# Moving the last routing steps and the zero fills in the planned order of a fused attention and expert kernel

## The chip, the cores and the metric

The kernel runs on one core of a Trainium2 chip. The metric is the device time in microseconds of one execution, 954.01 us before the change (median of three runs, 954.0 to 954.9). A profile of another execution of the same kernel shows where the time lies.

## What is computed

Three stages follow one another. The first is a recurrent attention with a complex decay per position, the second a mixture of eight experts of which every token goes to two, the third a feed-forward layer whose hidden value is the maximum of three products.

```python
# 4 batches, 8 heads, 768 positions, head size 48
scale = minimum(mag, 0.999) / (mag + 1e-06)
for t in range(768):
    S_re, S_im = ar * S_re - ai * S_im + k[t] v[t]^T, ar * S_im + ai * S_re
    y[t] = q[t] S_re
x = y as 3072 tokens x 384
noisy = x @ w_gate + log1p(exp(x @ w_noise)) * noise
top2, weights = two largest of noisy, softmax over them
out[token] += weight * (relu(x @ w1[e]) @ w2[e])        # 8 experts, 384 -> 1024 -> 384
h = maximum(maximum(x @ u1, x @ u2), x @ u3)            # 384 -> 768
result = h @ w_out
```

## The kernel before

The 3072 tokens are 24 chunks of 128, worked on in six sets of four chunks. For each set the decay (`gates`) is turned into cumulated magnitudes and angles: logarithms and exponentials with one table of ScalarE (tag `e1`), a matmul that cumulates and two exponentials of it, r and ri (tags `g`, `ex`), then arctangent and sine with another table (tags `t1`, `t2`, `f`, `sin`). For each chunk (`chunk`) q and k are scaled (`a0`, `a`), transposed (`b`), multiplied and masked (`d`), multiplied with v and the carried state (`c`, `s`, `l`); the output rows become fp16 pairs `xhl`, and logits of the gate come from the same product (`f_`).

Routing (`route`, tag `rt`) works on groups of two chunks, twelve groups. It finds the two experts of a token, counts tokens per expert with `acc`, and ends with `r2b3` (L900), which casts the row numbers into `sl`. A scatter (L940, tag `scat`, on POOL's queue) then writes the 128 rows of a chunk into the experts' row blocks in DRAM, two scatters per chunk, so four per group and 48 in all. Before any scatter, the row blocks are filled with zeros by eight fills of two transfers each on SP's queue (`zero_fill`, L972, tag `zf`).

The first pass of the experts (`first_pass`) takes 384 rows of each expert from chunks 0 to 11. Its weights (tag `xw`) are loaded once the `sl` of the fifth group is written, its rows are read by transposing transfers (tag `xx`, L1006) once the scatters of the first six groups are done. It is interleaved with the attention of chunks 12 to 23. The second pass (`second_pass`) takes the other 432 rows of each expert and needs all scatters. After it the third stage runs (`combine`, `hidden`, `last`), in a fixed order.

What sets the order up to the third stage is a planner inside the program, the class `Order`. Each step is added with a cost per engine, the keys it reads and writes, and a priority: the number of its chunk (or pass) plus an offset for its tag from the table `P["o"]`. The planner simulates the engines, their buffers and the ScalarE table phases: of the steps that are ready first it emits the one with the lowest priority. The order of emission is the order of instructions on each engine and each queue. On the chip only real data dependences make an engine wait; keys that exist for the planner alone shape the order, not the waits. Buffers limit it too: `xhl` has eight, `rw`, the scratch of routing, three.

The lines to watch are L900 (`sl`), L940 (scatters), L976 and L979 (zero fills), L437 (most ScalarE steps), L777 and L760 (state and output rows), L1037 and L1057 (first pass), L1098 and L1124 (second pass), L1507 (gathers of the third stage), L1557 and L1583 (its matmuls).

Of the kernel before, what the change touches and what calls it, by code (L numbers as in the profile page):

```python
# [32 lines left out]
    bufs=dict(bk=5, vg=2, wst=4, w1=1, w2=1, xa=2, hh=1, ya=2, ar=1, ai=1, iv=2, tn=1, r=1, ri=1, cs=3, fa=3,  # L33
           lam0=2, lam=6, lx=2, q=2, k=2, v=4, qr=3, kr=1, qc=2, kc=2, qt=2, kt=2, pm=2, xt=1, xhl=8, zp=1, fr=1,
           fh=4, car=1, sc=1, py=1, ps=1, lr=1, rw=3, w1b=1, w2b=1, raw=2, ua=1, vh=4, ch=1, cl=1),
    o=dict(load=-278.44, e1=-80.82, g=-44.76, ex=27.33, lam=13.6, t1=124.93, t2=491.73, f=-344.44, sin=58.57,
           tc=-621.27, qkv=204.29, v=669.22, a0=-227.64, a=84.82, b=-227.33, d=-609.19, c=-58.23, s=-165.23,
           l=90.33, f_=14.8, rt=-247.65, scat=-246.48, zf=803.51, gate=-153.95, noise=149.71, xw=125.96, xx=-312.17,
           x1=-201.57, xe=-424.5, x2=17.72, xo=-1189.75, yw=61.09, yx=-118.02, y1=-594.47, ye=185.57, y2=-134.08,
           yo=454.95, uw=1011.11, ue=388.46, pl=276.27, z=-83.6, mr=971.2),  # L40
    sets=[4, 4, 4, 4, 4, 4],
    e1ph=[0, 1, 2, 3, 4, 5],
    groups=[2, 2, 2, 2, 2, 2, 2, 2, 2, 2, 2, 2],
# [4 lines left out]
    a0=["dve"],  # L48
    a=["dve"],
# [11 lines left out]
    latpe=0.2,  # L61
    same=0.15,
    eps=0)
WARM = 20


class Order:
# [9 lines left out]
        self.bufs = bufs  # L77
        self.ops = []

    def add(self, fn, eng, prio, r=(), w=(), hold=(), table=None, phase=None, xfer=0.0, since=0, two=False, prev=None, mode=None, issues=1, after=()):  # L80

        self.ops.append(dict(fn=fn, eng=eng, prio=prio[0] + P["o"][prio[1]], r=list(r), w=list(w), hold=list(hold), table=table,
                             phase=phase, xfer=xfer, since=since, two=two, prev=prev, mode=mode, issues=issues, after=after))
        return len(self.ops) - 1

    def link(self):
# [32 lines left out]
    def run(self, emit, lat, latpe, same, eps):  # L121
# [14 lines left out]
        at = dict(self.BEGIN)  # L136
        hw = dma = awake = pe = port = done = 0.0
        mode = None
        need = {}
        for o in ops:  # L140
            if o["phase"] is not None:
                need[o["phase"]] = need.get(o["phase"], 0) + 1
        phase = 0
# [6 lines left out]
        while todo:  # L150
            best = None
            for e, ns in pool.items():
                cands = []
                for n in ns:
                    o = ops[n]
                    x = rdy[n][e]
                    if e in ("DVE", "POOL") and o["two"]:
                        x = max(x, port)
                    sw = False
                    if o["since"] > phase + (not need.get(phase, 0)):  # L160
                        continue
                    if o["table"] is not None:
                        if o["phase"] is not None and o["phase"] != phase:
                            if o["phase"] != phase + 1 or need.get(phase, 0):
                                continue
                            sw = True
                        elif o["phase"] is None and phase % 2:
                            if phase < end_phase or need.get(phase, 0):
                                continue
                            sw = True  # L170
                    ok = True
                    for t in o["tiles"]:
                        if t not in live:
                            f = free[self.CLASS.get(t[0], t[0])]
                            if not f:
                                ok = False
                                break
                            x = max(x, f[0][0])
                    if not ok:
                        continue  # L180
                    if sw:
                        x -= self.LOAD
                    cands.append((max(x, at[e]), o["prio"], n, sw))
                if not cands:
                    continue
                m = min(cands)[0]
                c = min((c for c in cands if c[0] <= m + eps), key=lambda c: (c[1], c[2]))
                if best is None or (c[0], c[1]) < best[0]:
                    best = (c[0], c[1]), e, c
            assert best, "too few buffers"  # L190
            _, e, (x, _, n, sw) = best
            o = ops[n]
# [6 lines left out]
            if e == "PE":  # L199

                if o["mode"] != mode:
                    mode = o["mode"]
# [5 lines left out]
                pe = x + cost  # L208
            end = x + cost
            at[e] = end  # L210
            if e in ("DVE", "POOL") and o["two"]:
                port = end
            if o["xfer"]:
# [35 lines left out]
def tile_kernel(ctx, tc, q, k, v, a_re, a_im, w_gate, w_noise, noise, w1, w2,  # L249
# [10 lines left out]
    E = w_gate.shape[1]  # L260
# [25 lines left out]
    ex = ctx.enter_context(tc.tile_pool(name="ex", bufs=1, side="left"))  # L286
# [89 lines left out]
    sl = const.tile([128, NI, 2], I32, name="sl")  # L376
# [7 lines left out]
    O = Order(BF)  # L384
# [437 lines left out]
    def route(gi, i0, n):  # L822
        sl_ = slice(i0, i0 + n)
        at, d = 0, {}
# [4 lines left out]
        def pr(x=0):  # L829
            return i0 + n - 1 + x, "rt"  # L830
# [91 lines left out]
        g = ("rt", i0, None)  # L922
# [6 lines left out]
        O.add(r1d, {"DVE": 0.08}, pr(1), r=[("rw", i0, 3)], w=[("rv", i0, "d")], hold=[("rw", i0)], two=True)  # L929
        O.add(r2b, {"DVE": 0.1}, pr(), r=[pp_], w=[("rw", i0, 8)])  # L930
        for m, (f, c) in enumerate(((r2b1, 0.2), (r2b2, 0.2), (r2b3, 0.08))):
            O.add(f, {"DVE": c}, pr(), r=[("rw", i0, m + 8)], w=[("sl", i0, None) if m == 2 else ("rw", i0, m + 9)], two=m == 0)
        O.add(r3, {"ACT": 0.1}, pr(1), r=[("rv", i0, "d")], w=[("rv", i0, 0)], hold=[("rw", i0)], table=0)
        for m, f in enumerate((r3b, r3c, r3d, r3e)):
            O.add(f, {"DVE": 0.08}, pr(1), r=[("rv", i0, m)], w=[("rv", i0, m + 1)], hold=[("rw", i0)], two=m in (0, 3))
# [15 lines left out]
        for j in range(n):  # L951
            for t in range(2):
                O.add(scatter(i0 + j, t), {"POOL": 1.26}, (i0 + j, "scat"),
                      r=[("sl", i0, None), ("xhl", i0 + j, None)] + [("xz", e, None) for e in range(E)], w=[("xs", i0 + j, t)], xfer=0.27)
# [382 lines left out]
    def combine_first(weighed):  # L1337
# [27 lines left out]
        for k in range(KD):  # L1365
# [17 lines left out]
          w=[("car", 1, None)])  # L1383
# [36 lines left out]
    def more_rows(e_, j):  # L1420
# [4 lines left out]
          w=[("wst", "no", None)])  # L1425
# [206 lines left out]
```

## Time and profile before

| | |
|---|---|
| median of three runs | 954.01 us (954.0 to 954.9) |
| span of the profiled execution, first to last instruction | 983.5 us |
| mean granted TensorE clock in it | 0.979 |
| busy: PE, DVE, ACT, POOL | 930.6, 574.0, 476.0, 139.0 us |
| instructions | 16814 |

The profiled execution is a run of its own, with a span 29.5 us above the median of the timed runs; the page gives no other time for it. PE is TensorE, DVE VectorE, ACT ScalarE, POOL GpSimd, and SP the queue that issues most transfers. A busy time counts from an instruction's start to its (for PE modelled) end. [...] "Idle before" is how long an engine did nothing ahead of an instruction, with what released it; "issue" means that nothing the profile shows was waited for, "remote" that the releaser isn't shown.

### The profile page before, as it was taken

Reading aid. Unit: us, or ns where it says so; the run is one execution under the profiler, and the core shown is the slowest. Engines: PE = TensorE matmul, PEld = TensorE weight load, DVE = VectorE, ACT = ScalarE, POOL = GpSimd, SP = SyncE. Lnnn points to the kernel's source line nnn. Section 1 sums busy time; section 2 is a strip of 40 time slices with the busy share of each in tenths; the row PEclk is TensorE's granted clock in tenths of the full one; section 3 lists DMA queues with packets and bytes.
Section 4 is the critical chain, followed back from the end, with each engine's and each line's share of the span. In section 5 each row is a group of like instructions: output and inputs, shape, how many; then the busy total and the mean of one; then the engine's idle time right before and its main releaser. Section 6 shows DMA issues by size and latency. Waiting matters only on the chain. (4 is left out here: it accounts for less than half of the span.)

```text
span 983.5 us, 16814 instructions
## 1 busy us (share of the span) xinstructions
PE 930.6 (95%) x6312; PEld 586.8 (60%) x6312; DVE 574.0 (58%) x1252; ACT 476.0 (48%) x922; POOL 139.0 (14%) x197
## 2 busy tenths in 40 slices
PE   3989778899999999899999999999799999999998
PEld 1868667787666766455555555555675445454544
DVE  5989748999655756565887764454344332424231
ACT  7998748978644556243445444333233132313221
POOL 0101442422001000520100000000433030300000
PEclk9999969999999999899999999999999999999999
DMA  9999848796765546379888785552335141502000
GB/s 150 211 214 271 195 120 159 182 194 165 191 185 168 158 153 201 123 223 312 253 253 238 209 208 155 147 141 79 107 116 142 40 133 36 140 25 78 25 9 33
DMA packets 247902, 150.98 MB, mean 154 GB/s; under 512 B 196488, under 2 KB 235528, under 8 KB 247816
## 3 DMA queue, kind: packets, MB, share of 16 engines
q1 hardware_dynamic: 241672, 130.98, 52.1%
q0 software_dynamic: 6144, 18.88, 6.4%
q8 instruction: 50, 0.82, 0.4%
q14 instruction: 36, 0.29, 0.1%
HBM read 89.78 MB, written 45.81 MB: 138 GB/s over the span
## 5 line engine op out<-in xcount | busy, mean ns | idle before, releaser
L437 ACT ACTIVATE hh<-bk 128x384 f16<-128x384 f32 (+1 forms) x128 | 64.6, 508 | 85.4 <-PE bk L1098 43.2
L985 ACT ACTIVATE w<-wst 128x768 f16<-128x768 f32 (+1 forms) x77 | 71.1, 932 | 59.6 <-PE bk L1057 23.3
L1057 PE MATMUL bk<-w,hh 128*128 128x384 f16 x576 | 98.6, 331 | 1.3 <-issue 1.3
L1037 PE MATMUL bk<-xa,w 128*128 128x384 f16 x576 | 99.6, 326 | 0.0
L987 DVE SCALAR_TENSOR_TENSOR w<-wst,w 128x768 f16<-128x768 f32 (+1 forms) x77 | 81.4, 1068 | 12.4 <-ACT w L985 11.5
L1571 ACT ACTIVATE th<-mx 128x512 f16<-128x512 f32 (+1 forms) x42 | 23.8, 568 | 127.2 <-DVE mx L1570 125.5
L1057 PEld LDWEIGHTS <-hh 128*128 128x128 f16 x576 | 56.7, 99 | 41.6 <-issue 6.5
L1124 PEld LDWEIGHTS <-hh 128*128 128x128 f16 x576 | 55.0, 98 | 40.3 <-issue 5.0
L1037 PEld LDWEIGHTS <-w 128*128 128x128 f16 x576 | 55.1, 98 | 34.4 <-issue 1.4
L1569 DVE TENSOR_TENSOR mx<-mx,u 128x512 f32<-128x512 f32 (+1 forms) x42 | 25.6, 610 | 62.5 <-PE u L1557 62.5
L1507 POOL DMA_INDIRECT yg<-ys_rows,sy x42 | 43.5, 1036 | 119.6 <-ACT za L1511 104.4
L940 POOL DMA_INDIRECT xs_rows<-xhl,sl x48 | 55.4, 1154 | 35.5 <-issue 18.5
L443 DVE COPY ya<-bk 128x384 f32<-128x384 f32 x37 | 20.6, 558 | 67.7 <-PE bk L1057 45.7
L732 PE MATMUL sc<-qt,kt 96*128 96x128 f32 x384 | 55.4, 287 | 4.5 <-issue 1.8
L732 PEld LDWEIGHTS sc<-qt,kt 96*128 96x128 f32 x384 | 49.3, 197 | 12.1 <-issue 4.1
L1098 PE MATMUL bk<-xa,w1b 128*128 128x432 f16 x288 | 53.2, 346 | 0.0
L1098 PE MATMUL bk<-xa,w 128*128 128x432 f16 x288 | 53.2, 346 | 0.0
L1107 DVE SCALAR_TENSOR_TENSOR hh<-bk,hh 128x432 f16<-128x432 f32 x64 | 37.9, 605 | 24.9 <-ACT hh L437 24.8
L1124 PE MATMUL bk<-w2b,hh 128*128 128x384 f16 x288 | 48.4, 326 | 0.0
L1124 PE MATMUL bk<-w,hh 128*128 128x384 f16 x288 | 48.4, 326 | 0.0
L1570 DVE TENSOR_TENSOR mx<-mx,u 128x512 f32<-128x512 f32 (+1 forms) x42 | 25.7, 611 | 37.4 <-PE u L1557 33.2
L1513 DVE SCALAR_TENSOR_TENSOR z<-yg,wt,za 128x384 f32<-128x384 f32 x22 | 12.8, 614 | 58.7 <-ACT za L1511 52.2
(204 smaller groups left out, 2012.7 us busy)
## 6 DMA issues: line engine op xcount, KB each, us to landing
wst<-in_moe_w_dram SPq DMA_DIRECT2D x45, 512.0 KB
wst<-in_moe_w_dram SPq DMA_DIRECT2D x60, 384.0 KB
xs_rows<-wst SPq DMA_DIRECT2D x8, 1152.0 KB
ys_rows<-ya SPq DMA_DIRECT2D x48, 192.0 KB
raw<-in_moe_w_dram SPq DMA_DIRECT2D x9, 768.0 KB
ar<-in_a_re_dram SPq DMA_DIRECT2D x24, 192.0 KB
ai<-in_a_im_dram SPq DMA_DIRECT2D x24, 192.0 KB
q<-in_q_dram SPq DMA_DIRECT2D x24, 192.0 KB
```

The source lines that it names most:

```text
L437: nc.scalar.activation(o, i, f, **kw)
L732: nc.tensor.matmul(tl("sc", (i, g))[:, j, :], tl("kt", i)[:, h, :], tl("qt", i)[:, h, :], start=True, stop=True)
L940: ins = nc.gpsimd.indirect_dma_start(out=xs, out_offset=bass.IndirectOffsetOnAxis(ap=sl[:, i, t:t + 1], axis=0), in_=tl("xhl", i), in_offs ...
L985: nc.scalar.activation(hi, src, AF.Copy, scale=scale)
L987: nc.vector.scalar_tensor_tensor(lo, src, scale, hi, op0=OP.mult, op1=OP.subtract)
L1037: nc.tensor.matmul(tl(*b)[:, :RA], tl("w1", e)[:, w, k, f * 128:(f + 1) * 128], tl("xa", e)[:, x + k, :RA], start=(k == m == 0), stop=(k = ...
L1057: nc.tensor.matmul(tl(*b)[:, :HD], tl("hh", e)[:, a, f, t * 128:(t + 1) * 128], tl("w2", e)[:, w, f], start=(f == m == 0), stop=(f == KF - ...
L1098: nc.tensor.matmul(tl(*b)[:, :RB], tl(n1, inst)[:, w, k, f * 128:(f + 1) * 128], tl("xa", xi)[:, x + k], start=(k == m == 0), stop=(k == K ...
L1107: nc.vector.scalar_tensor_tensor(tl("hh", xi)[:, 1, f], tl(*b)[:, :RB], 0.0, tl("hh", xi)[:, 0, f], op0=OP.max, op1=OP.subtract)
L1124: nc.tensor.matmul(tl(*b)[:, :HD], tl("hh", xi)[:, a, f, ts_], tl(n2, inst)[:, w, f], start=(f == m == 0), stop=(f == KF - 1 and m == 2))
L1507: nc.gpsimd.indirect_dma_start(out=y, out_offset=None, in_=src, in_offset=bass.IndirectOffsetOnAxis(ap=row[:, i, s:s + 1], axis=0))
L1570: nc.vector.tensor_tensor(a, a, ps[2], op=OP.max)
```

## The change

Four things change. The cast `r2b3` (L900) also reads the keys `xz` of all eight zero fills, so the planner puts it behind them. It also gets a pace: the planner lets two such casts start no less than `APART` = 14 us apart on its own clock. The offsets of all tags are replaced by others. The constant `WARM`, which nothing uses, is gone. No instruction is added or removed; the order of the instructions changes on every engine up to the third stage.

```diff
--- before.py
+++ after.py
@@ -33,11 +33,12 @@
     bufs=dict(bk=5, vg=2, wst=4, w1=1, w2=1, xa=2, hh=1, ya=2, ar=1, ai=1, iv=2, tn=1, r=1, ri=1, cs=3, fa=3,
            lam0=2, lam=6, lx=2, q=2, k=2, v=4, qr=3, kr=1, qc=2, kc=2, qt=2, kt=2, pm=2, xt=1, xhl=8, zp=1, fr=1,
            fh=4, car=1, sc=1, py=1, ps=1, lr=1, rw=3, w1b=1, w2b=1, raw=2, ua=1, vh=4, ch=1, cl=1),
-    o=dict(load=-278.44, e1=-80.82, g=-44.76, ex=27.33, lam=13.6, t1=124.93, t2=491.73, f=-344.44, sin=58.57,
-           tc=-621.27, qkv=204.29, v=669.22, a0=-227.64, a=84.82, b=-227.33, d=-609.19, c=-58.23, s=-165.23,
-           l=90.33, f_=14.8, rt=-247.65, scat=-246.48, zf=803.51, gate=-153.95, noise=149.71, xw=125.96, xx=-312.17,
-           x1=-201.57, xe=-424.5, x2=17.72, xo=-1189.75, yw=61.09, yx=-118.02, y1=-594.47, ye=185.57, y2=-134.08,
-           yo=454.95, uw=1011.11, ue=388.46, pl=276.27, z=-83.6, mr=971.2),
+    o=dict(a=1997.92, a0=-6086.53, b=-20253.93, c=-899.72, d=-23372.44, e1=-6277.48, ex=11220.71, f=-1274.0,
+           f_=-5017.85, g=1136.97, gate=-3606.18, l=1201.84, lam=-493.0, load=-5446.23, mr=14034.07, noise=-968.55,
+           pl=906.65, qkv=-496.01, rt=-20910.65, s=-10552.53, scat=-3329.6, sin=-4552.9, t1=-195.74, t2=-2593.92,
+           tc=-29968.09, ue=11614.6, uw=26447.45, v=54.69, x1=-14968.92, x2=-1209.51, xe=-381.58, xo=-2174.31,
+           xw=3235.52, xx=-2356.48, y1=-2393.16, y2=-479.64, ye=-1286.59, yo=-1086.56, yw=490.14, yx=238.25,
+           z=1781.12, zf=1230.22),
     sets=[4, 4, 4, 4, 4, 4],
     e1ph=[0, 1, 2, 3, 4, 5],
     groups=[2, 2, 2, 2, 2, 2, 2, 2, 2, 2, 2, 2],
@@ -61,7 +62,7 @@
     latpe=0.2,
     same=0.15,
     eps=0)
-WARM = 20
+APART = 14.0
 
 
 class Order:
@@ -77,12 +78,12 @@
         self.bufs = bufs
         self.ops = []
 
-    def add(self, fn, eng, prio, r=(), w=(), hold=(), table=None, phase=None, xfer=0.0, since=0, two=False, prev=None, mode=None, issues=1, after=()):
+    def add(self, fn, eng, prio, r=(), w=(), hold=(), table=None, phase=None, xfer=0.0, since=0, two=False, prev=None, mode=None, issues=1, after=(), pace=None):
 
 
 
         self.ops.append(dict(fn=fn, eng=eng, prio=prio[0] + P["o"][prio[1]], r=list(r), w=list(w), hold=list(hold), table=table,
-                             phase=phase, xfer=xfer, since=since, two=two, prev=prev, mode=mode, issues=issues, after=after))
+                             phase=phase, xfer=xfer, since=since, two=two, prev=prev, mode=mode, issues=issues, after=after, pace=pace))
         return len(self.ops) - 1
 
     def link(self):
@@ -136,6 +137,7 @@
         at = dict(self.BEGIN)
         hw = dma = awake = pe = port = done = 0.0
         mode = None
+        paced = {}
         need = {}
         for o in ops:
             if o["phase"] is not None:
@@ -178,6 +180,8 @@
                             x = max(x, f[0][0])
                     if not ok:
                         continue
+                    if o["pace"] is not None:
+                        x = max(x, paced.get(o["pace"][0], -1e9) + o["pace"][1])
                     if sw:
                         x -= self.LOAD
                     cands.append((max(x, at[e]), o["prio"], n, sw))
@@ -208,6 +212,8 @@
                 pe = x + cost
             end = x + cost
             at[e] = end
+            if o["pace"] is not None:
+                paced[o["pace"][0]] = x
             if e in ("DVE", "POOL") and o["two"]:
                 port = end
             if o["xfer"]:
@@ -929,7 +935,8 @@
         O.add(r1d, {"DVE": 0.08}, pr(1), r=[("rw", i0, 3)], w=[("rv", i0, "d")], hold=[("rw", i0)], two=True)
         O.add(r2b, {"DVE": 0.1}, pr(), r=[pp_], w=[("rw", i0, 8)])
         for m, (f, c) in enumerate(((r2b1, 0.2), (r2b2, 0.2), (r2b3, 0.08))):
-            O.add(f, {"DVE": c}, pr(), r=[("rw", i0, m + 8)], w=[("sl", i0, None) if m == 2 else ("rw", i0, m + 9)], two=m == 0)
+            O.add(f, {"DVE": c}, pr(), r=[("rw", i0, m + 8)] + ([("xz", e, None) for e in range(E)] if m == 2 else []),
+                  w=[("sl", i0, None) if m == 2 else ("rw", i0, m + 9)], two=m == 0, pace=("sl", APART) if m == 2 else None)
         O.add(r3, {"ACT": 0.1}, pr(1), r=[("rv", i0, "d")], w=[("rv", i0, 0)], hold=[("rw", i0)], table=0)
         for m, f in enumerate((r3b, r3c, r3d, r3e)):
             O.add(f, {"DVE": 0.08}, pr(1), r=[("rv", i0, m)], w=[("rv", i0, m + 1)], hold=[("rw", i0)], two=m in (0, 3))
```

## Rows read from the trace of the kernel before

**Rows 1.** The page's head and first part: busy us, share of the span, instructions.

```profile
span 983.5 us, 16814 instructions
...
PE 930.6 (95%) x6312; PEld 586.8 (60%) x6312; DVE 574.0 (58%) x1252; ACT 476.0 (48%) x922; POOL 139.0 (14%) x197
```

**Rows 2.** Windows: stretch, length, busy us of each engine, granted clock, DMA share, GB/s.

```profile
25.00:113.00 88.00, 80.88 (x761) 68.53 (x760) 78.14 (x220) 81.42 (x182) 12.83 (x15) 0.96 1.04 227
...
113.00:145.00 32.00, 23.93 (x181) 20.16 (x180) 16.33 (x51) 16.56 (x37) 18.78 (x35) 0.73 0.45 129
...
120.50:132.50 12.00, 4.99 (x17) 2.67 (x18) 1.08 (x7) 2.95 (x8) 8.47 (x16) 0.72 0.49 164
...
145.00:235.00 90.00, 81.90 (x829) 69.68 (x828) 83.55 (x235) 77.44 (x168) 27.70 (x40) 0.98 0.88 183
...
401.60:416.00 14.40, 10.78 (x53) 5.20 (x50) 4.99 (x10) 1.74 (x3) 9.09 (x18) 0.76 0.47 158
...
460.00:690.00 230.00, 229.35 (x1420) 127.56 (x1419) 142.32 (x201) 94.93 (x150) 6.12 (x6) 1.00 0.66 192
...
690.00:746.00 56.00, 50.75 (x392) 39.45 (x391) 20.70 (x49) 16.01 (x40) 18.78 (x19) 0.94 0.43 112
...
746.00:983.00 237.00, 233.78 (x1173) 114.58 (x1171) 77.68 (x122) 62.23 (x113) 25.37 (x24) 1.00 0.22 65
```

**Rows 3.** Timeline of POOL: start us, us, line, operation, idle time before, its releaser.

```profile
114.96 1.16 POOL L940 DMA_INDIRECT xs_rows<-xhl,sl  x1 [1.48 <-issue]
...
129.46 0.96 POOL L940 DMA_INDIRECT xs_rows<-xhl,sl  x1 [0.22 <-issue]
...
396.80 1.01 POOL L940 DMA_INDIRECT xs_rows<-xhl,sl  x1 [3.12 <-DVE rw L893]
...
411.87 0.96 POOL L940 DMA_INDIRECT xs_rows<-xhl,sl  x1 [0.21 <-issue]
```

**Rows 4.** Timeline of PE, DVE, ACT and SP in the two bursts, same columns.

```profile
119.30 0.37 SPq L703 DMA_DIRECT2D k<-in_k_dram  x1
...
132.41 10.61 SPq L704 DMA_DIRECT2D vb<-in_v_dram  x2
...
132.48 0.60 ACT L441 ACTIVATE xt<-py 128x512 f16<-128x512 f32 x1 [7.79 <-remote]
...
132.48 0.55 DVE L777 TENSOR_TENSOR mb<-mb,ps 96x384 f32<-96x384 f32 x1 [8.84 <-remote]
...
402.49 0.32 PE L750 MATMUL py<-pm,vb 128*64 128x128 f32 x1 [0.39 <-issue]
...
403.20 0.27 PE L753 MATMUL py<-qt,mb 96*64 96x128 f32 x1 [0.38 <-issue]
```

**Rows 5.** Windows of two single groups of four scatters.

```profile
164.00:176.00 12.00, 7.99 (x60) 7.28 (x59) 11.49 (x25) 10.83 (x24) 10.37 (x9) 0.86 0.74 198
...
186.00:193.00 7.00, 6.74 (x80) 6.03 (x78) 6.85 (x17) 6.51 (x17) 5.68 (x9) 1.00 0.79 165
```

**Rows 6.** Timeline: a slot cast and the last zero fill.

```profile
61.12 0.16 DVE L900 CAST sl<-slf 128x4 int32<-128x4 f32 x1
...
108.05 0.60 SPq L976 DMA_DIRECT2D xs_rows<-wst  x1
```

**Rows 7.** Single lines in stretches: durations, then first and last start.

```profile
L900 DVE CAST sl<-slf x2: 164/468/773, 164.0 to 185.6; 128x4 int32<-128x4 f32 x2
...
L900 DVE CAST sl<-slf x4: 161/176/253, 396.4 to 433.2; 128x4 int32<-128x4 f32 x4
```

**Rows 8.** Timeline of SP: first row transpose of the second pass.

```profile
454.10 1.65 SPq L1006 DMA_TRANSPOSE xa<-xs_rows  x1
```

**Rows 9.** Single lines: expert matmuls of either pass, durations, first and last start.

```profile
L1037 PE MATMUL bk<-xa,w x576: 322/326/337, 207.4 to 457.5; 128*128 128x384 f16 x192
...
L1098 PE MATMUL bk<-xa,w x288: 346/346/346, 469.5 to 646.5; 128*128 128x432 f16 x144
```

**Rows 10.** Group of instructions by form: busy us, mean ns, idle before.

```profile
L437 ACT ACTIVATE r<-bk 128x384 f32<-128x384 f32 x24 | 11.8, 492 | 1.6 <-PE bk L554 1.4
```

## The prediction

> **What bounds the kernel now.** I read the page's totals first: PE is busy 930.6 of 983.5 us [rows 1], so the time is PE's work plus the stretches in which PE lacks work, stalls or runs at its lower clock. The windows show where [rows 2]. From 746 to 983 us PE is busy 233.78 of 237, from 460 to 690 us 229.35 of 230: nothing to gain there. From 25 to 113 and from 145 to 235 us ACT (81.42 of 88) and DVE (83.55 of 90) are as full as PE (80.88, 81.90): this is the attention stage, where three engines share the limit and a lost microsecond is lost for all. Two stretches stand out. From 113 to 145 us DVE is busy only 16.33 of 32 at a mean granted clock of 0.73, and from 120.5 to 132.5 us DVE 1.08 and ACT 2.95 of 12. From 401.6 to 416 us PE is busy 10.78 of 14.4 at 0.76.
>
> The POOL timeline says what is special there [rows 3]: twelve scatters of rows (L940), each about 1 us, run from 114.96 to 130.4 us, 1.3 us apart, and twelve from 396.80 to 412.8 us. In the first burst DVE waits 8.84 us and ACT 7.79 us for something "remote", and SP, whose preceding transfer was issued at 119.30 us, issues its next one at 132.41; in the second PE issues one matmul every 0.7 us without a named wait [rows 4]. Groups of four scatters, as from 186 to 193 us (PE 6.74 of 7), do no such harm [rows 5]. So the harm comes with the length of the burst.
>
> The bursts have two causes. The slots (L900) of group 0 were ready at 61.12 us, but every scatter must follow all eight zero fills, the last issued at 108.05 us [rows 6]; so groups 0 to 2 are let go at once. Groups 8 to 10 are routed together: their slots come from 396.4 us on, and the last group's at 433.2 [rows 7].
>
> **The change, part by part.** (1) The slot cast of every group now comes after the zero fills in the planner's order, and two casts are at least 14 us apart on the planner's clock. No instruction is added or removed: 12 casts, 48 scatters, 16 zero-fill transfers stay. What moves is the cast on DVE, and behind it on POOL its four scatters (4 x 1.3 = 5.2 us [rows 3]) and the POOL operations between them. On SP nothing waits for the cast except the expert weights (after group 4's) and the row transposes of the two passes.
>
> First burst: 16.33 us of DVE work at the 0.90 busy share of its two neighbours (78.14 of 88 and 83.55 of 90 [rows 2]) would take 18.1 us, so 32 - 18.1 = 13.9 us are lost. Not all of it can move the gate of the first expert pass: with the first cast at about 113 us (the first scatters follow the zero fills there) and five steps of 14 us, group 5's slots come at 183 us, against 185.6 before [rows 7]. The gate moves by 2.6 us; the other 11.3 us become attention work done before the gate, worth 11.3 x 0.92 (PE's busy share from 25 to 113 us) = 10.4 us of later PE time. Sum 13; ends 2.6 and 13.9.
>
> [...] Three steps of 14 us put the last group's slots at 396.4 + 42 = 438.4 us, 5.2 us later than 433.2. This is hidden: the rows of the second pass are first transposed at 454.10 us and first used at 469.5 us [rows 8, 9], 15 us of cover; without that cover it would cost up to 5.2 us, and more if PE arrives earlier.
>
> (2) The offsets are all new. What counts is the rank per engine, as chunk numbers differ by a few tens at most and most offsets by hundreds. On SP zero fills stay behind q, k and v, but weights (xw) fall from before q, k, v to behind them and behind the zero fills; on DVE the sine chain (f) drops from fourth to ninth, behind the routing, a0 and e1; on ACT the exponentials of the cumulated sums (ex) drop from the middle to last but one. No row prices this. On the gaining side it can at most fill PE's other idle time between 25 and 235 us, 7.1 + 8.1 = 15.2 us [rows 2]; on the losing side the nearest row is a set boundary that goes badly, 164 to 176 us, where PE is busy 7.99 of 12 [rows 5]: 4 us each, three boundaries in the attention stage, 12 us. I take 0, as neither end is nearer to a row of the new order.
>
> Sum against the profiled execution: 13 + 7 = 20 us, 983.5 to 963.5. The median of the runs, though, is 954.0, which is 29.5 us below the span, and PE's rate from 460 to 690 and after 746 us leaves no room for an excess. It must lie in the idle stretches. The stalls behind long runs of POOL transfers add up to nearly that: 13.9 + 7.0, and a third after ten gathers, from 690 to 746 us, where PE idles 5.25 us and runs 56 x 0.06 = 3.4 us short of clock [rows 2]. That is 29.5 us. So perhaps the timed runs have little of these stalls: the gain lies between 0 and 20 us. I take 30% of it, 6 us, because the agreement of the two sums speaks for small stalls, while other idle time before 235 us could hold part of the excess instead.
>
> The rows show the engines at a standstill and name no cause [rows 4]. [...]
>
> **The rivals.** *Nothing to gain:* the stalls belong to the profiled execution, or the gate (183 against 185.6 us) holds and the attention work done ahead meets full buffers. For it: the two sums of 29.5 us. Against: ACT, DVE and PE all have idle time from 25 to 113 us too, and it could hold part of the excess. Time 954.
>
> *Slower through the exponentials:* r and ri, two instructions of 0.49 us per chunk [rows 10], eight per set, now come behind nearly all that ACT has ready. q and k can't be scaled without them, and the table can't be switched to the sine set. ACT is busy 93% from 25 to 113 us, so its list rarely empties and ex waits until it does; it decides when ACT is above some 90% at a boundary. Price as above: 4 us at each of three boundaries, 12 us, against the 6 gained: 960. For it: the full ACT. Against: an exponential that others wait for leaves those others unready, which empties the list by itself.
>
> *The change doesn't do what it says:* the 14 us are the planner's, and the scatters wait on the chip for the zero fills' landing, which the planner only estimates. If the fills land 28 us later than planned, three groups pile up on POOL as before: 954, give or take the new order.
>
> **How the numbers follow.** Bursts gone and part of the stall real: 0.50, at 948 (934 to 952). Nothing to gain: 0.18, 954. Exponentials: 0.22, 960 (956 to 966). Not as it says: 0.10, on both sides of 954: 0.03 faster, 0.03 same, 0.04 slower. A measurement here tells 0.2%, 1.9 us, from no change. Faster: 0.53; same: 0.21; slower: 0.26. The likeliest case is 948. The range leaves one in ten at each end: 935 to 963; the likeliest case's own is 934 to 952.
>
> **What would show it.** Right: in the changed profile no more than four to six scatters in a row on POOL, the first behind the zero fills; no 8 us "remote" waits on DVE and ACT near 120 us; SP without a gap of 13 us; PE without 0.7 us steps near 400 us; the clock near 1 in both stretches; the first expert matmul no later than 207 us [rows 9]. If all this is there, the span falls by more than the median does. Wrong: bursts of eight or more; slots of group 5 later than 190 us; ACT or PE waits of several microseconds before r and ri; a gap on PE at the start of the second pass. If the span falls by 20 us and the median by 20 as well, the stalls were real in the timed runs and my 30% is the failed step.

## The result, and the profile after

| kernel | time, median (lowest to highest) | span of its profile | ratio to before, 95% interval |
|---|---|---|---|
| before | 954.35 us (954.0 to 956.89, 5 runs) | 983.5 us | |
| changed | 967.87 us (961.2 to 969.19, 5 runs) | 967.4 us | 1.0117 [1.0086, 1.0148] |

The change made the kernel slower by 13.5 us where the forecast said 6 us faster, and 967.9 lies above the forecast's upper end of 963. Yet the span of the profile fell by 16 us. Both are true, and the reason is the main finding: the profile of before [rows 1] and the timed runs of before were not of one kind. In the experiments below the kernel before ran on six chips. On four of them it took 954.7 to 957.4 us, on two 983.4 and 984.0 us; the changed kernel, run beside it on three of the six, took 964.6 to 968.8 us on either kind.

Most of what the forecast wanted to see in the changed profile is there. First the page's head, then the POOL timeline (start us, us, line, operation, idle time before, its releaser): the first scatter of four groups, and the last scatter of all.

```profile
span 967.4 us, 16805 instructions
...
PE 924.2 (96%) x6312; PEld 582.4 (60%) x6312; DVE 577.5 (60%) x1254; ACT 476.1 (49%) x917; POOL 143.0 (15%) x200
```

```profile
106.67 1.16 POOL L947 DMA_INDIRECT xs_rows<-xhl,sl  x1 [6.35 <-DMA ar<-in_a_re_dram]
...
123.95 1.01 POOL L947 DMA_INDIRECT xs_rows<-xhl,sl  x1 [1.08 <-DVE sl L906]
...
267.98 1.01 POOL L947 DMA_INDIRECT xs_rows<-xhl,sl  x1 [25.03 <-DVE zp L805]
...
379.26 1.01 POOL L947 DMA_INDIRECT xs_rows<-xhl,sl  x1 [2.20 <-ACT w L992]
...
426.98 0.96 POOL L947 DMA_INDIRECT xs_rows<-xhl,sl  x1 [0.21 <-issue]
```

No more than four scatters stand in a row, where [rows 3] has twelve twice; the 8 us "remote" waits and the 0.7 us steps of [rows 4] are gone: no wait of DVE or ACT is put down to "remote" any more, and from 400 to 416 us PE is busy 16.00 of 16 us at a granted clock of 1.00.

To see where 13.5 us went, the kernel before needs a profile without standstills (stretches like that from 120.5 to 132.5 us in [rows 2], in which PE, DVE and ACT do little). The experiment `e1_before` gave one: a span of 953.9 us. In the windows of 100 to 250 us (length, busy us of PE, PEld, DVE, ACT, POOL, granted clock, DMA share, GB/s; the clock is a share, 1.00 the highest in any window here) it and the changed kernel differ most; first `e1_before`, then changed:

```profile
100.00:250.00 150.00, 139.26 (x1291) 112.81 (x1290) 132.61 (x364) 126.67 (x271) 57.48 (x82) 0.97 0.82 191
```

```profile
100.00:250.00 150.00, 134.37 (x1262) 111.02 (x1262) 128.66 (x377) 119.38 (x258) 60.92 (x93) 0.94 0.72 169
```

PE is idle 15.6 us instead of 10.7, and 0.03 less clock over 150 us is by estimate another 4.5 us: 9.4 us of the loss. Among PE's groups of instructions the largest single difference is the sine chain's cumulating matmul (busy us, mean ns, idle us before and its releaser; before, then changed), 3.8 us of idle time and 3.8 of busy time, part of them in the same stretch:

```profile
L635 PE MATMUL bk<-tn,ut 128*128 128x384 f32 x48 | 21.4, 541 | 3.4 <-ACT tn L437 3.4
```

```profile
L641 PE MATMUL bk<-tn,ut 128*128 128x384 f32 x48 | 25.2, 628 | 7.2 <-ACT tn L443 7.2
```

The loss is complete when the second expert pass begins, whose first 72 matmuls start 11.8 us later (before, changed); PE has no wait from 400 to 500 us in the changed kernel, and the rest of the program, from there to the end, takes 507.7 and 509.5 us.

```profile
446.18 13.30 PE L1098 MATMUL bk<-xa,w 128*128 128x432 f16 x72
```

```profile
457.94 13.30 PE L1105 MATMUL bk<-xa,w 128*128 128x432 f16 x72
```

### The profile page after: what moved, and what is told of

It is laid out like the page before. It is cut to its first block, busy times and chain, and to the rows that moved or that the text cites. A ratio compares the mean times of both kernels' runs of the same rounds, so it can differ in the third digit from the quotient of the medians.

```text
span 967.4 us, 16805 instructions
## 1 busy us (share of the span) xinstructions
PE 924.2 (96%) x6312; PEld 582.4 (60%) x6312; DVE 577.5 (60%) x1254; ACT 476.1 (49%) x917; POOL 143.0 (15%) x200
## 5 line engine op out<-in xcount | busy, mean ns | idle before, releaser
L1064 PE MATMUL bk<-w,hh 128*128 128x384 f16 x576 | 95.2, 326 | 0.0
L947 POOL DMA_INDIRECT xs_rows<-xhl,sl x48 | 57.5, 1198 | 84.2 <-DVE zp L805 29.2
L1576 DVE TENSOR_TENSOR mx<-mx,u 128x512 f32<-128x512 f32 (+1 forms) x42 | 25.6, 609 | 61.0 <-PE u L1564 60.8
L1053 DVE SCALAR_TENSOR_TENSOR hh<-bk,hh 128x384 f16<-128x384 f32 x64 | 35.1, 552 | 23.5 <-ACT hh L443 23.1
L1131 PE MATMUL bk<-w,hh 128*128 128x384 f16 x288 | 48.4, 326 | 0.0
## 6 DMA issues: line engine op xcount, KB each, us to landing
wst<-in_moe_w_dram SPq DMA_DIRECT2D x45, 512.0 KB
```

The costliest lines, as they stand in the source:

```text
L947: ins = nc.gpsimd.indirect_dma_start(out=xs, out_offset=bass.IndirectOffsetOnAxis(ap=sl[:, i, t:t + 1], axis=0), in_=tl("xhl", i), in_offs ...
L1064: nc.tensor.matmul(tl(*b)[:, :HD], tl("hh", e)[:, a, f, t * 128:(t + 1) * 128], tl("w2", e)[:, w, f], start=(f == m == 0), stop=(f == KF - ...
L1131: nc.tensor.matmul(tl(*b)[:, :HD], tl("hh", xi)[:, a, f, ts_], tl(n2, inst)[:, w, f], start=(f == m == 0), stop=(f == KF - 1 and m == 2))
```

## Experiments: the parts of the change

**The kernel before, once more** (`e1_before`, no edit).

> The kernel before, looked at again. Its first profile has a span of 983.5 us, 29.5 above its timed runs, while the changed kernel's span (967.4) is 1.8 below its own time. If the stalls behind twelve scatters come with the recording, the span is again near 983 and the same stretches (120 to 132 us, 402 to 408 us) stand still. If they come and go by chance, the span is near 952, the stretches are full, and the first second-pass matmul (469.5 us before) starts near 443.

955.69 us (one run), span 953.9: both rows of twelve scatters are there, from 115.78 and from 381.55 us, and neither stops PE, which from 380 to 400 us is busy 20.00 of 20 us. In the stretch of the first (compare the same window in [rows 2]: PE 23.93, DVE 16.33, granted clock 0.73):

```profile
113.00:145.00 32.00, 31.60 (x349) 28.64 (x347) 28.94 (x93) 28.72 (x66) 22.36 (x38) 0.99 0.88 219
```

So the long row of scatters is not enough for a standstill, and a profiled execution needn't have one.

**Zero fills first, nothing else** (`e4_fills_first_old`).

```diff
-            O.add(f, {"DVE": c}, pr(), r=[("rw", i0, m + 8)],
+            O.add(f, {"DVE": c}, pr(), r=[("rw", i0, m + 8)] + ([("xz", e, None) for e in range(E)] if m == 2 else []),
```

> The old offsets, slots behind the zero fills, but no pace between them (0 us instead of 14). Theory A: 950 to 956. Theory B with the pace as the cost: 954, against 963 to 970 with the pace; theory B with the zero fills as the cost: both 963 to 970.

956.69 us, ratio 1.0002 [0.998, 1.0023]. With the old offsets this part costs nothing.

**Zero fills and pace, with the offsets of before** (`e2_pace_old_offsets`), and **the new offsets alone** (`e3_new_offsets_only`: `APART = 0.0`, no `xz` keys).

> Only the zero fills ahead of the slots and the 14 us pace; the old offsets. Theory A (the new offsets cost the time): 950 to 956, no slower than before. Theory B (holding the slots back costs the time, because expert weights and the first pass wait for groups 4 and 5): 963 to 970, like the whole change.

> Only the new offsets; slots free of the zero fills and of the pace. Theory A: 963 to 970. Theory B: 950 to 956. If both parts are needed for the loss (the offsets were made for the paced order), both this and the paced kernel with old offsets are nearer to 954 than to 968.

998.2 us, ratio 1.0421 [1.0378, 1.0465], and 981.91 us, 1.0255 [1.0215, 1.0295]. Each alone is worse than both together, so neither is *the* cause: the new offsets win back some 30 of the 42 us that the pace costs with the old ones. The waits of PE from 400 to 500 us (us in total, times, longest) say how the two differ. In `e2_pace_old_offsets`, with the last slot cast at 454.43 us:

```profile
PE bk L1104 <- DMA xa<-xs_rows: 25.5, 5, 9.7
```

The last groups' slots come one pace after the other from 415 us on, and PE stands ahead of the second pass with no rows, 25.5 us in all; between these waits it works at a lower clock, 0.81 in the mean from 400 to 500 us (12 matmuls of the second pass take 4.48 us from 485.82 us on, where 72 take 13.30 us in `e1_before`). In `e3_new_offsets_only`:

```profile
PE bk L1044 <- ACT w L992: 4.8, 1, 4.8
PE bk L1064 <- ACT w L992: 2.3, 1, 2.3
PE bk L1044 <- DVE w L994: 1.8, 2, 1.4
PE bk L1064 <- DVE w L994: 1.1, 2, 0.7
```

Here the slots are early (the last from 396.6 us), but the weights of the first pass's last expert are late: 10.0 us. PE's mean granted clock is 0.93 in this window, as it is from 100 to 250 us (0.979 over the whole execution, against 0.994 in `e1_before`), so those 10 us are only a part of the 25.

**The pace on half of the groups, old offsets** (`e5_pace_first_six`, `e6_pace_last_six`).

```diff
-   pace=("sl", APART) if m == 2 else None)
+   pace=("sl", APART) if m == 2 and gi < 6 else None)     # e6: gi > 5
```

> Old offsets, slots behind the zero fills, and the pace of 14 us for the first six groups of chunks alone. Theory H (the held first six slots cost the time): in the undisturbed look at the kernel before, the sixth slot cast starts at 170.2 us and the second pass of the experts at 446.2; in the changed kernel 183.9 and 457.9. If this shift of 13.7 and 11.8 us is the pace's own, it comes back here without any new offset: the second pass starts at 456 to 460 and the time is about 954.4 + 12 = 966 us. Theory R (the new offsets' order makes the loss in the first 250 us; for example the first expert's weights asked for at 165.8 instead of 149.4 us): the first pass starts as in the kernel before and the time stays within 957 us.

> Old offsets, slots behind the zero fills, and the pace for the last six groups alone. The pace on all twelve groups with old offsets cost 42 us, of which 33 us stood ahead of the second pass, where TensorE waits for the transposed rows of the last groups. Theory H: those 33 us stay and the first part goes, so 954.4 + 42 - 12 = 984 us, with a gap at the start of the second pass. Theory R: the whole 42 us belong to the last six groups, 996 us. A third way: the last six only took long because they started late, after the first six had been held, and four groups at 14 us can be caught up: under 965 us.

964.72 us, ratio 1.0082 [1.0056, 1.0107], and 974.0 us, 1.0173 [1.0146, 1.02]. The first half alone, with no new offset, gives what the changed kernel gives; its second pass starts at 457.24 us, also like the changed kernel's. The second half costs 18.3 us by itself, of which PE waits

```profile
PE bk L1104 <- DMA xa<-xs_rows: 11.0, 3, 5.8
```

and the sum of the halves, 27 us, is 14 us short of the 42: with the first six held as well, the last cast comes at 454 instead of about 428 us.

**The pace on the last six groups, new offsets** (`e7_new_pace_last_six`), and **new offsets without pace but with the two old offsets `ue` and `uw`** (`e9_new_no_pace_old_u`).

> The changed kernel, but the pace only for the last six groups, so the first six are free as in the kernel before. Theory H: the sixth slot cast comes back from 183.9 to about 170 to 175 us, the second pass starts at 446 to 450 and the time is 967.9 - 12 = 956 us. Theory R: the new offsets still ask for the first expert's weights late and leave TensorE idle until 240 us, 967 us as the changed kernel. A third way: the offsets were fitted to the paced order of all twelve, and without it the order falls apart as in the run with new offsets and no pace, 980 us.

> The new offsets without any pace (981.9 us), but the two offsets of the output layer's weights (ue, uw) as in the kernel before. In that run TensorE stood idle 10.4 us between 430 and 462 us, waiting for expert weights that ScalarE and VectorE convert, while SyncE's queue waited 12.0 us behind loads of the output layer (raw) for their buffer. If those two offsets pull the loads ahead and this makes the gap, it goes: 981.9 - 10.4 - 1.4 of low clock = 970 us. If the gap has another cause (the last slots' time, the order of the experts' weights xw themselves), the time stays at 980 to 984 us.

Both runs keep the zero-fill keys, which `e3_new_offsets_only` hasn't. 1009.32 us, ratio 1.0561 [1.0528, 1.0594], and 1008.32 us, 1.0537 [1.0512, 1.0562]. Both expectations fell. In `e7_new_pace_last_six` the last two groups are scattered from 455.6 us on, and PE waits from 400 to 500 us:

```profile
PE bk L1105 <- DMA xa<-xs_rows: 28.0, 5, 10.3
```

The slot casts of the two runs nearly agree, though one has the pace on its last groups and the new `ue` and `uw`, the other no pace and the old ones. First `e3_new_offsets_only`, then these two (casts after 300 us: count, durations in ns, first and last start in us):

```profile
L906 DVE CAST sl<-slf x2: 159/164/170, 367.8 to 396.6; 128x4 int32<-128x4 f32 x2
```

```profile
L906 DVE CAST sl<-slf x4: 152/165/170, 327.2 to 461.0; 128x4 int32<-128x4 f32 x4
```

```profile
L906 DVE CAST sl<-slf x4: 154/165/171, 330.6 to 464.4; 128x4 int32<-128x4 f32 x4
```

So neither the two offsets nor the pace on the last groups explains the last casts. Against `e3_new_offsets_only` the two runs share one edit, the zero-fill keys: with the new offsets and the first six groups unpaced they go with some 26 us more, where `e4_fills_first_old` shows them free with the old offsets. (No run adds them to `e3_new_offsets_only` alone.) The price of a part depends on the offsets it meets.

**Half the pace** (`e8_new_apart7`, `e18_new_apart7_again`: `APART = 7.0` in the changed kernel).

> The changed kernel with a pace of 7 us instead of 14, on all twelve groups. Theory H alone: five steps of 7 us are 35, so nothing is held, the sixth slot cast comes at 165 to 175 us and the time is 956 us. Theory F (the new offsets fit the paced order and no other; with the last six groups alone paced they gave 1009 us and with none 982): the order falls apart again, 980 us or more, with TensorE waiting ahead of the second pass.

> The changed kernel with a pace of 7 us, again. It took 987.3 us on the chip where the kernel before takes 984. It has no row of more than four scatters there, so by theory S only about 7 us of that are the chip's: where the kernel before takes 955 us, theory F (the new offsets fit the pace of 14 us alone) gives 980 us; theory H alone gave 956.

987.3 and 987.32 us, ratios 1.0022 [0.9999, 1.0044] and 1.0045 [1.0022, 1.0067]; both fell on chips where the kernel before takes 984 us. PE is idle 24 and 27 us between 100 and 250 us at mean clocks of 0.90 and 0.91. Part of that looks like the hazard itself: no row has more than four scatters, but sixteen of them run from 106 to 142 us with 5 to 7 us from the last of a four to the next, and in both runs ScalarE again waits for something the profile doesn't name (the second run, from 100 to 250 us: us in total, times, longest; in the first 4.9 and 3.1 us), where neither `e1_before` nor the changed kernel on such a chip has any such wait:

```profile
ACT xt L447 <- remote: 4.9, 1, 4.9
ACT qt L447 <- remote: 3.0, 1, 3.0
```

Theory H isn't tested here: it forecast the sixth cast at 165 to 175 us, and it stands at 187.68 and 183.64, about where 14 us put it (183.92, and 186.27 on such a chip), although five steps of 7 us are 35. How much of the 31 us above 956 is the standstills' and how much the offsets' was not separated, since neither run fell on a chip without them. The half pace is no better than the kernel before, and 18.6 us behind the whole pace on the same chip.

## Experiments: what the held slots hold

The paced first half costs about 10 us. Two things read the slots there: the first expert's weight loads, planned behind the fifth cast, and the row transposes, which need the sixth group's scatters.

**A pace of 11 us on the first six groups, old offsets** (`e11_first_six_11us`, `e14_first_six_11us_again`: `APART = 11.0` in `e5_pace_first_six`).

> The run with the pace on the first six groups (964.7 us) at 11 us instead of 14. Without a pace and behind the zero fills the first slot cast stood at 117.3 and the sixth at 171.9 us, 54.6 apart. Theory H (the pace costs what it moves the sixth group): five steps of 11 us are 55, so the sixth stays at 172 to 174 and the time is 956 us. If the pace costs by disturbing the order at any size, the time lies between, 960 to 965 us.

> The pace of 11 us on the first six groups with the old offsets, again, to have it on a chip without standstills. Where the kernel before takes 955 us: theory H (the pace costs what it moves the sixth group, and five steps of 11 us are the 54.6 us that the slots take without a pace) 956 us; if the pace costs by disturbing the order, 960 to 965 us. Where the kernel before takes 984 us it should repeat 985 us.

On a chip where the kernel before takes 954.7 us: 965.03 us, ratio 1.0112 [1.0085, 1.0139]. (On one where it takes 984.0: 985.35, ratio 1.0007.) The sixth cast stands at 176.13 us, against 170.19 before and 189.88 with 14 us, and the cost is about the same at both (10.3 and 9.1 us). So the cost is not simply what the sixth group is moved by; the second case of the expectation held.

What is alike in both is the sixth transpose of rows on SP's queue, with which the first expert's rows are complete: it is issued at 208.48 us in `e1_before`, 217.64 with 11 us, and second of the pair at 219.06 with 14 us (start us, time on the queue, operation, count):

```profile
208.48 1.12 SPq L1006 DMA_TRANSPOSE xa<-xs_rows  x1
```

```profile
217.64 2.42 SPq L1012 DMA_TRANSPOSE xa<-xs_rows  x2
```

```profile
219.06 2.54 SPq L1012 DMA_TRANSPOSE xa<-xs_rows  x2
```

With six free slots the six transposes start at 181.99 us and are spread over 26 us between other loads; with 11 us they start at 188.76 and are spread over 29, with 14 us at 201.22 and over 19. Until they are there, PE has only the attention's chunks to work on. In `e1_before` 49 matmuls of the first expert run from 220 to 230 us, in the changed kernel 12, and its block comes 20 us later (busy us and count, clock):

```profile
220.00:230.00 10.00, 8.14 (x49) 1.00 0.39 116
```

```profile
220.00:230.00 10.00, 2.45 (x12) 1.00 0.65 179
...
240.00:250.00 10.00, 7.48 (x45) 1.00 0.78 180
```

**Weights released earlier** (`e10_first_six_w_early` on the paced first half with old offsets; `e12_after_w_early`, `e16_after_w_early_again` on the changed kernel).

```diff
-        weigh(e, "w1", "w2", e, pr("xw"), [("sl", ends[GA - 2], None)])
+        weigh(e, "w1", "w2", e, pr("xw"), [("sl", ends[GA - 4], None)])
```

> The run with the pace on the first six groups (964.7 us), but the first pass's weight loads are released in the plan by the third group's slots instead of the fifth's. In that run the first weight load was asked for at 170.2 us and the first transposed rows at 201.2; in the undisturbed look at the kernel before at 149.4 and 182.0. Theory W (the held slots cost the time because the first expert's weights are planned behind the fifth slot cast): the weights come back before 160 us, TensorE is full from 220 us again and the time is 957 us. Theory X (the rows set it: every first-pass transpose needs the scatters of the sixth group): the time stays at 964 to 966 us. If weights that come early only take ScalarE's and VectorE's time from the chunks' work, it is slower than 966.

> The changed kernel (967.9 us), but the first pass's weight loads are released in the plan by the third group's slots (137.6 us) instead of the fifth's (169.3). Theory W: first weight load before 150 us, TensorE full from 225 us, 957 to 960 us. Theory X (rows): 966 to 969 us. Theory F (any other order makes the new offsets fall apart): 980 us or more.

> The changed kernel with the first pass's weights released by the third group's slots, again. It took 976 us where the kernel before took 984. Where the kernel before takes 955 us: theory W (the late weights hold the first pass) 956 to 960 us; theory X (the transposed rows hold it) 964 to 968 us, as the changed kernel. Where the kernel before takes 984 us it should repeat 976 us, and stands beside the changed kernel itself: equal by theory X, 8 us or more better by theory W.

The changed kernel with early weights took 968.7 us, ratio 1.0118 [1.0092, 1.0145], beside 964.6 us for the changed kernel on the same chip. Its first weights are converted at 143.98 us instead of 175.47, and nothing is gained: the late weights are not what holds the first pass. But its sixth transpose is issued at 212 us, only 4 us later than before, and it loses 11 us all the same. So late rows fit the paced runs with old offsets, where they aren't shown to be the cause, and not this one. That holding the first six slots costs about 10 us with the old offsets is shown; that it is the same cost in the changed kernel is inferred from the like times (second pass from 457.24 and 457.94 us), and by which chain of small waits between 150 and 250 us is open.

## Experiments: two kinds of chips

On the chip of `e8`, `e10`, `e11` and `e12` the kernel before took 984.0 us (976.8 to 988.82, 25 runs). There the early weights on the changed kernel gave 976.07 us, faster than before: 0.9906 [0.9871, 0.9942]; the paced first half with early weights 982.68, 0.9991 [0.9971, 1.0011]. The second of these keeps the twelve scatters in a row near 400 us. In its windows of 2 us (length, busy us of PE, PEld, DVE, ACT, POOL, clock, DMA share, GB/s), PE falls idle from the fifth scatter on (401.29 us), DVE and ACT follow, and the granted clock drops to 0.50:

```profile
400.00:402.00 2.00, 1.06 (x19) 0.94 (x15) 0.02 (x1) 2.00 (x3) 1.75 (x3) 1.00 0.60 208
402.00:404.00 2.00, 0.75 (x5) 0.29 (x4) 2.00 (x7) 0.20 (x1) 1.56 (x5) 0.87 0.32 118
404.00:406.00 2.00, 0.45 (x1) 0.28 (x2) 1.63 (x3) 0.00 (x0) 1.78 (x3) 0.50 0.64 141
406.00:408.00 2.00, 1.14 (x4) 0.38 (x4) 0.00 (x0) 0.00 (x0) 1.42 (x5) 0.50 0.97 307
```

The same twelve scatters in `e1_before`, on a chip where before takes 956.5 us, with PE full throughout:

```profile
386.00:388.00 2.00, 2.00 (x26) 1.45 (x23) 2.00 (x3) 1.52 (x2) 1.55 (x5) 1.00 0.51 147
388.00:390.00 2.00, 2.00 (x15) 1.22 (x13) 2.00 (x3) 0.00 (x0) 1.77 (x3) 1.00 0.88 207
390.00:392.00 2.00, 2.00 (x14) 1.22 (x13) 0.67 (x2) 0.00 (x0) 1.78 (x3) 1.00 1.03 310
```

That made it a question of chips, and the changed kernel was run beside the kernel before on three more (`e13_after_again`, `e15_after_third`, `e17_after_fourth`; no edit).

> The changed kernel once more, beside the kernel before on the same chip. In the last runs the kernel before took 984.0 us on one chip (25 runs) against 955 to 957 us on three others, and 984 is what its first profile showed with the standstills behind long rows of scatters. Theory S (the standstills are a property of the chip): on a chip where the kernel before takes about 984 us, the changed kernel has lost its rows of eight to twelve scatters, keeps its loss of 12 us in the first pass's gate and takes 970 to 976 us, so a ratio of 0.985 to 0.992; on a chip where the kernel before takes 955 us there is nothing to save and the ratio is 1.010 to 1.015 again. Theory T (that chip is slower at everything by 3 per cent): the ratio is 1.01 on either.

> The changed kernel beside the kernel before on one more chip. Theory S (standstills behind rows of eight or more scatters belong to some chips): if the kernel before takes about 984 us here, the changed kernel takes 970 to 976 us, a ratio of 0.985 to 0.992; if it takes 955 us, the ratio is 1.010 to 1.015 as on the last chip (1.0104). Theory T (such a chip is slower at everything): 1.01 on either.

> The changed kernel beside the kernel before once more. Where the kernel before takes about 984 us: theory S 972 us (its 965 us elsewhere and the 7.4 us by which the kernel with its early weights was longer there), a ratio of 0.988; theory T 994 us. Where the kernel before takes 955 to 957 us: 962 to 968 us.

| chip | before | changed | ratio |
|---|---|---|---|
| of e13 | 954.69 (7 runs) | 965.5 (4) | 1.0104 [1.0087, 1.0121] |
| of e15 | 957.39 (11) | 964.6 (8) | 1.008 [1.0049, 1.011] |
| of e17 | 983.43 (13) | 968.76 (2) | 0.9862 [0.9823, 0.99] |

Theory T fell; theory S held in its ratios (1.008 is a little under its range), but not in blaming the long rows alone. Where the kernel before takes 983 us, the changed one is faster by 14.7 us; elsewhere it loses 7 to 11, and 13.5 in the result above. By kernel, the difference between the two kinds of chips falls with the rows of twelve scatters: two rows (before) +28 us, one row (11 us pace, 985.35 against 965.03) +20, none (changed with early weights, 976.07 against 968.7) +7, the changed kernel itself +1 to +4.

Not all of it is theirs. With the 11 us pace the second pass starts 18.3 us later on the disturbed chip (`e11_first_six_11us`, then `e14_first_six_11us_again`):

```profile
472.34 13.30 PE L1104 MATMUL bk<-xa,w 128*128 128x432 f16 x72
```

```profile
454.05 13.30 PE L1104 MATMUL bk<-xa,w 128*128 128x432 f16 x72
```

The row near 400 us accounts for about 6 us of that, an estimate (from 400 to 420 us PE is busy 16.64 against 19.19 us at a clock of 0.83 against 1.00). A part of the rest lies from 100 to 250 us, where only fours stand (130.19 against 133.70 us busy, 0.91 against 0.97). And behind the start of the second pass, where no scatter runs, `before` still takes 514.0 us [rows 1, 9] and `e1_before` 507.7, the changed kernel 512.0 (`e17_after_fourth`) and 509.3 to 509.5 us. There ten gathers of the third stage follow one another 1.25 us apart, in `before` from 695.70 and in the changed kernel from 683.61 us, the third stall that the prediction priced; the change doesn't touch them. In `e12_after_w_early` DVE waits beside them, from 680 to 720 us, for something unnamed, 4.0 us; the profile of the changed kernel in the result above has no such wait:

```profile
DVE mx L1576 <- remote: 4.0, 1, 4.0
```

In the profile of e17 the window that lost 13.9 us in [rows 2] shows the changed order at work:

```profile
113.00:145.00 32.00, 30.32 (x324) 26.73 (x325) 30.04 (x89) 26.38 (x60) 16.72 (x24) 1.00 0.72 156
```

No version here beats both kernels on both kinds. Why two chips of six behave so was not shown.

## Why the prediction failed

**What bounds the kernel** was read from one execution of one kind and set against a median of the other. That the 29.5 us between them were the standstills was right, nearly in the parts too: without them the second pass starts 23.3 us earlier (469.5 to 446.18, against 13.9 + 7.0 in the sum), and what follows is 6.3 us shorter (against 8.65 for the third stall). The 7.0 us of the second burst can be read from [rows 2]: 3.6 us in which PE does nothing, and 14.4 us at a mean granted clock of 0.76, which in windows of 2 us is 0.50 from 406 to 412 us. No run shows this loss by itself; for such a row the 11 us pace gave about 6 us, the estimate above.

**The term that failed** is the weight of 30%. It treated the 20 us as a quantity of which some share is real. It is nearly all or nothing by chip: on the chip with standstills where both kernels ran the change nets 14.7 us; on the others there is nothing to save, and the sum should have held 0 and the losses alone. Both times of before were given with a reading for each, "timed runs have little of these stalls" and "the stalls were real", and the forecast took a value between them at which neither lies.

**The gate of the first pass** failed with it. 183 us for the sixth cast was good (183.92), but it was compared with 185.6 [rows 7], which the first standstill had delayed. In an execution without it the cast stands at 170.19:

```profile
170.19 0.98 DVE L900 CAST sl<-slf 128x4 int32<-128x4 f32 x1
```

```profile
183.92 0.15 DVE L906 CAST sl<-slf 128x4 int32<-128x4 f32 x1
```

So "2.6 us earlier" was 13.7 us later. The mark set for being wrong, slots later than 190 us, rested on the same row and didn't trip. The sign of being right, the first expert matmul no later than 207 us, rested on that execution as well: 207.6 us nearly met it, against 192.1 in `e1_before`. The price, about 10 us, is what `e5_pace_first_six` shows for this part alone, with the old offsets.

**The last group's slots** were put at 438.4 us and covered by 15 us [rows 8, 9]. In the changed kernel they come at 421.7 and PE has no gap, so the outcome is as forecast, but not for the reason given: the new offsets route groups 8 and 9 more than 100 us earlier (scatters from 268 and 282 us against 381.6 and 386.7 in `e1_before`). The cover was misread: the transfer at 454.10 us [rows 8] is the fourth row transpose of the second pass. The first follows the last scatter:

```profile
441.73 1.12 SPq L1006 DMA_TRANSPOSE xa<-xs_rows  x1
```

What is covered shows when the slots are held with the old offsets (`e6_pace_last_six` against `e1_before`): the last cast comes 17.7 us later, PE reaches the second pass 4.3 us later and still waits 11.0 us for rows. By these numbers some 2 us were covered (an estimate), not 15, and the hold cost 18.3 us in all.

**The offsets** were taken as 0, with ends of -15.2 and +12. They are worth about -30 us with the keys and the pace, and +25 without both. Both ends were far too near, since they were built from idle time and boundaries of the old order.

**The rivals.** "Nothing to gain" was right for these runs but had no cost in it. "Slower through the exponentials" had the side and nearly the place, not the mechanism: in the changed kernel other engines waited 0.2 us for r in all, and PE, from 100 to 250 us, 1.9 us for a transfer from ri, against 4.8 in `e1_before`. Their arctangent neighbours do show, as the 3.8 us of idle time ahead of the sine chain's matmul, and that is a part of the loss at most. "Doesn't do what it says" fell: the first scatters follow the zero fills, and casts stand 13.4 us or more apart.

**Recording, and the cause.** If the stalls belonged to the profiled execution, recording would make them. Recording alone doesn't, as the profiled execution of `e1_before` has both rows of scatters and no standstill (PE busy 31.60 of 32 us beside the first row, 20.00 of 20 beside the second). Whether recording takes part on the chips with standstills is open: every run here, the timed ones too, has a recorded span and clock, so none is known to be unrecorded. What stops the engines no run here shows. That only real data dependences make an engine wait isn't shown either: DVE's 8.84 and ACT's 7.79 us [rows 4] are put down to "remote", and the steps of 0.7 us on PE to nothing named.

## What to carry to other kernels

When a profile's span and the timed runs differ by more than a few microseconds, get a second execution before reading any time from the first: a standstill moves every later time (here the sixth cast to 185.6 us from 170.19), so a step that is "no later than before" may be late. Price a hold at its reader in the undisturbed order, and with the planner's table of offsets unchanged and changed, since here zero-fill keys and pace cost 42 us with the old table, while with the new one the kernel took 14 us less with them than without. A change that removes a hazard is worth what the hazard costs on the chip at hand: here some 25 us (28 less the 1 to 4 that stayed), or nothing.

## What the hardware showed unexpectedly

On two of six chips the kernel before took 28 us more than on the other four, with the same program. Where profiles show it (the first one, and `e10` and `e11` on one of the two chips), a row of twelve indirect scatters of 128 rows each, 1.3 us apart, goes with a stretch of some microseconds in which PE, DVE and ACT run dry: in `e10`, PE is busy 0.45 of 2 us from 404 us on and DVE and ACT 0.00 from 406. In it the granted clock falls to 0.50, and DMA moves 118 and 141 GB/s in two of the windows shown. In `e1_before`, on another chip, PE is busy 20.00 of 20 us beside such a row. On a disturbed chip fours that begin 5 to 7 us behind the last of the four before still show waits of 3 to 5 us (`e8`, `e18`: 4.9 and 3.0 to 3.1 us of ACT, 3.5 of DVE); in the changed kernel's order, with 9 us or more, no such wait shows (`e17`), and PE's idle time from 100 to 250 us is 17.7 us on such a chip against 13.0 to 15.6 in three profiles on others. Scatters aren't the only case: behind the start of the second pass, where ten gathers stand in a row, 2.6 to 6.3 us more go by on such chips.
